# A fused attention and gated convolution kernel: the third weight unit loaded behind the first pair's queries and keys, with 30 GpSimd steps tied to VectorE

## The chip, the cores and the metric

The kernel runs on one core of a Trainium2 chip. The core has five engines with instruction queues of their own: TensorE (PE in the profile; PEld is its loading of weights), VectorE (DVE), ScalarE (ACT), GpSimd (POOL) and SyncE (SP), which here issues the transfers. The metric is the device time of one execution in microseconds. Of the kernel before, three runs are shown.

## What is computed

Attention inside chunks of 64 tokens, for 8 batches, 8 heads, 576 tokens and a head size of 64; its output, as rows of 512 numbers, goes through a causal convolution of five taps with a sigmoid (the gate), is multiplied by a weight matrix (the value), and the product of gate and value is multiplied by a second weight matrix:

```python
scores = scale * np.matmul(q_c, k_c.transpose(0, 1, 2, 4, 3))   # chunks of 64
scores = scores - np.max(scores, axis=-1, keepdims=True)
attn = np.exp(scores)
attn = attn / (np.sum(attn, axis=-1, keepdims=True) + 1e-09)
x = np.matmul(attn, v_c)                                        # then B x 576 x 512
for k in range(K):                                              # K = 5
    gate_pre += conv_w[k][None, None, :] * xp[:, k:k + S, :]
gate = 1.0 / (1.0 + np.exp(-gate_pre))
val = x @ w_val
return (gate * val @ w_out).astype(np.float32)
```

q, k and v are float32. The two weight matrices (512 x 512) and the taps are float64.

## The kernel before

**Tiling.** The 4608 tokens are cut into nine groups g of 512. In each group the eight heads make two pairs p of 128 partitions. Queries, keys and values of one (g, p) are 512 KB each, one tile of 128 x 1024 each; group 0's queries and keys of both pairs 0 1 and 0 0 come in halves b of 256 KB (S, mx and the like have a third number then). A weight matrix comes as four units of 128 rows, `v 0` to `v 3` of w_val and `o 0` to `o 3` of w_out, 512 KB each, since they are float64.

**What sets the order.** The program is one string, ORDER, of 1034 pieces. A loop takes them one by one and calls the function of each name; `run` (L138, L139, so every instruction of the kernel shows line L139) keeps this order on every engine. So each engine goes through its own instructions in the order of the string, waits where an input isn't ready, and what stands behind on that engine waits too. A table SLOTS says for every tile that a piece makes, one after the other, which buffer it takes: z for the 38 buffers of 128 x 1024 in SBUF, b for the four double banks of PSUM, e for two rows of exponentials. Buffers with a number from ALONE = 20 on lie in one tensor, `ys`; two neighbours there can be worked on by one instruction, where the code asks for a pair.

**The pieces.** `lq`, `lk`, `lv` load queries, keys and values of (g, p); `lw` loads a weight unit, `lc` the taps. All loads are issued by SP, in order. A weight unit's bits are turned on the chip into two float32 parts (`v_hi`, `v_lo`, `o_hi`, `o_lo`), in steps: w1, w3, w4, w7 on VectorE, w2, w5 and w6 on ScalarE, w8, wa and wb on GpSimd. Where `Q` is listed (`v 1`, `v 2`, `v 3`), the low part is summed on PE by three matmuls instead (wa and wb fall away) and copied by `wc` on ScalarE. A suffix D puts a step on VectorE, G on GpSimd.

For a pair: `S` makes scores on PE, `mx` their maxima (VectorE), `sb` subtracts (VectorE), `ex` is the exponential (ScalarE), `sm` sums and takes the reciprocal (VectorE), `nm` normalises (GpSimd), `T` transposes (PE), `ec` copies (ScalarE), `A` multiplies by the values (PE). There are two other ways to the exponentials. `ng` and `ea`: one exponential for each block of 64 on ScalarE, with the maximum as bias and the sum accumulated by it, 16 instructions for a pair and 8 for a half (`ra` and `rr`, or `rc`, then add a small number and invert). And `mh`, `M`, `exM`: the maxima in two parts (VectorE), subtracted on PE by matmuls into the scores, then one exponential out of PSUM.

`xr` and `xd` split the attention output into two parts (ScalarE, VectorE), `xc` copies it for the convolution, `k0`, `k`, `kk`, `kx` are taps, `sg` the sigmoid (ScalarE). `V g m c` is one contraction step of the value product, three matmuls of 512 columns (hi x hi, lo x hi, hi x lo); `vc` copies the value, `gs` multiplies it with the gate, `gr` and `gd` split that product, `P g m c` is a step of the out product, `oc` copies it and `st` stores. `W` are matmuls on zeros, `zr`, `zi`, `zw`, `zs` set constants up.

**Lines that matter here.** SLOTS and ALONE (L100), `run` (L138), `lw` (L183), `w1` (L203), `sc`, which is S (L261), `less`, which is M (L321), `exm` (L329) and the dispatch (L599 to L610).

## Time and profile before

| | |
|---|---|
| runs | 280.51, 281.16, 281.65 us (median 281.16) |
| span of the profiled execution | 279.6 us (of this execution the page gives the span alone) |
| PE busy | 268.9 us, 96% of the span, 3370 matmuls |
| PE loading weights | 216.6 us, 77% |
| VectorE busy | 239.5 us, 86%, 303 instructions |
| ScalarE busy | 198.7 us, 71%, 368 instructions |
| GpSimd busy | 59.4 us, 21%, 58 instructions |
| transfers | 42.46 MB, mean 152 GB/s |
| the chain that ended last | PE 89%, DMA 8% of the span |

The shares are means over the whole span. The page also has the span in 40 slices of 7 us; in it the second and third slice show PE at 5 and 9 tenths with transfers at 395 and 409 GB/s, and nearly every later slice shows PE at 9 tenths. So the table is read together with the chain of waits, which tells in which stage PE waits for transfers, and in which PE follows on itself.

### The profile page before, as it was taken

The numbers are of one execution on the slowest core, as the hardware profiler recorded it, in microseconds if no ns is written. First come the engines' busy times: TensorE is split into PE (matmuls) and PEld (weight loads), VectorE is DVE, ScalarE is ACT, GpSimd is POOL, SyncE is SP. The second block draws the span as 40 slices with busy tenths as digits, with TensorE's granted clock in tenths as the row PEclk, the third lists the DMA queues.
The fourth block names the chain that finished last, engine by engine and source line by source line (L and its number), as shares of the span: only waits on it lengthen the run. The fifth ranks groups of instructions, "written<-read, shape, count | busy, mean of one in ns | idle before, by whom it ended". The sixth has DMA issues, their size and how long they took to land.

```text
span 279.6 us, 7851 instructions
## 1 busy us (share of the span) xinstructions
PE 268.9 (96%) x3370; PEld 216.6 (77%) x3370; DVE 239.5 (86%) x303; ACT 198.7 (71%) x368; POOL 59.4 (21%) x58
## 2 busy tenths in 40 slices
PE   6598999999998999999999999999999999999995
PEld 3366778887886888888888888888888888888884
DVE  3979999999999988989898998999999998996020
ACT  5899999999997988895958588837644544614402
POOL 1056242049294003061335001100000000300000
PEclk9999999999999999999999999999999999999999
DMA  6999999763831649540082000000000000050656
GB/s 224 395 409 406 406 407 409 290 225 108 281 149 37 192 150 338 189 131 30 2 292 88 2 5 2 0 0 2 0 0 0 4 0 0 16 212 0 241 209 225
DMA packets 14754, 42.46 MB, mean 152 GB/s; under 512 B 1536, under 2 KB 1792, under 8 KB 14720
## 3 DMA queue, kind: packets, MB, share of 16 engines
q1 hardware_dynamic: 14720, 41.97, 40.7%
q8 instruction: 26, 0.43, 0.6%
q14 instruction: 8, 0.07, 0.1%
HBM read 32.53 MB, written 9.44 MB: 150 GB/s over the span
## 4 chain that ended last, share of the span: by engine, by line
PE 89%; DMA 8%; issue 1%; SPq 0%; ACT 0%
PE b L139 89%; DMA z<-in_v 4%; DMA z<-in_moe_w_val 2%; DMA z<-in_q 2%; SPq L139 0%; ACT z L139 0%
## 5 line engine op out<-in xcount | busy, mean ns | idle before, releaser
L139 PE MATMUL b<-z,v_hi 128*128 128x512 f32 x288 | 97.3, 403 | 1.3 <-issue 1.1
L139 PE MATMUL b<-o_hi,z 128*128 128x512 f32 (+1 forms) x296 | 94.5, 391 | 0.0
L139 DVE SCALAR_TENSOR_TENSOR ys<-ys,cw 128x511 f32<-128x511 f32 (+7 forms) x104 | 84.5, 863 | 0.1
L139 ACT COPY z<-b 128x1024 f32<-128x1024 f32 (+2 forms) x53 | 50.3, 970 | 38.3 <-PE b L139 35.5
L139 PEld LDWEIGHTS b<-z,v_hi 128*128 128x128 f32 x288 | 53.8, 188 | 14.5 <-issue 1.7
L139 PEld LDWEIGHTS b<-o_hi,z 128*128 128x128 f32 x296 | 55.1, 188 | 12.6
L139 PE MATMUL b<-o_lo,z 128*128 128x512 f32 (+1 forms) x148 | 57.4, 388 | 0.0
L139 PE MATMUL b<-z,v_lo 128*128 128x512 f32 x144 | 55.9, 394 | 0.0
L139 POOL TENSOR_TENSOR z<-e_row,rs 128x1024 f32<-128x1024 f32 (+1 forms) x15 | 27.0, 1804 | 47.2 <-DVE rs L139 17.0
L139 PEld LDWEIGHTS b<-o_lo,z 128*128 128x128 f32 x148 | 27.8, 188 | 5.9
L139 PEld LDWEIGHTS b<-z,v_lo 128*128 128x128 f32 x144 | 27.1, 188 | 5.4
L139 POOL TENSOR_TENSOR z<-ys,z 128x1024 fp32r<-128x1024 f32 x4 | 10.0, 2527 | 96.9 <-ACT z L139 96.9
L139 ACT ACTIVATE ys<-ys 128x1024 f32<-128x1024 f32 x16 | 16.8, 1059 | 11.0 <-DVE ys L139 10.8
L139 ACT ACTIVATE e_row<-b,mx 128x64 f32<-128x64 f32 x80 | 23.7, 345 | 0.4 <-DVE mx L139 0.4
L139 DVE TENSOR_TENSOR z<-b,z 128x1024 fp32r<-128x1024 f32 (+1 forms) x19 | 22.0, 1161 | 2.3 <-ACT z L139 1.3
L139 ACT CAST z<-ys 128x1024 fp32r<-128x1024 f32 x16 | 16.5, 1048 | 9.0 <-DVE ys L139 9.0
L139 DVE TENSOR_REDUCE mx<-b 128x16 f32<-128x1024 f32 (+1 forms) x19 | 21.6, 1144 | 1.3 <-PE b L139 1.1
L139 PEld LDWEIGHTS b<-z,z 64*64 64x64 f32 x960 | 15.7, 135 | 7.8 <-DMA z<-in_k 2.6
L139 PE MATMUL b<-z,z 64*64 64x64 f32 x960 | 17.6, 221 | 3.7 <-DMA z<-in_q 3.0
L139 ACT CAST z<-b 128x1024 fp32r<-128x1024 f32 (+1 forms) x19 | 18.7, 991 | 2.1 <-PE b L139 2.1
L139 ACT ACTIVATE ys<-ys,cw 128x512 f32<-128x512 f32 (+1 forms) x25 | 19.2, 811 | 0.0
L139 ACT ACTIVATION_READ_ACCUMULATOR e_row<-b,mx 128x1 f32 x80 | 19.0, 238 | 0.0
(74 smaller groups left out, 308.3 us busy)
## 6 DMA issues: line engine op xcount, KB each, us to landing
out<-z SPq DMA_DIRECT2D x16, 512.0 KB, 3.7
z<-in_q SPq DMA_DIRECT2D x10, 512.0 KB, 7.2
z<-in_v SPq DMA_DIRECT2D x9, 512.0 KB, 5.0
ys<-in_v SPq DMA_DIRECT2D x9, 512.0 KB, 10.1
ys<-in_k SPq DMA_DIRECT2D x9, 512.0 KB, 7.3
z<-in_k SPq DMA_DIRECT2D x7, 512.0 KB, 9.4
ys<-in_q SPq DMA_DIRECT2D x6, 512.0 KB, 10.2
z<-in_moe_w_val SPq DMA_DIRECT2D x4, 512.0 KB, 5.4
```

The lines of the kernel that those rows point to most:

```text
L139: return tc.keep_in_program_order(fn(*args, **kwargs))
```

## The change

The order string has 1033 pieces. The first 328 of them (up to about a third of the span) stand in another order than the first 329 of before; the last 705 are the same. What differs:

- `lw v 2`, the load of the third weight unit, stood third among the units; it now stands behind all queries and keys of the pairs 0 1 and 0 0. `lw v 0`, `lk 1 1` and `lq 1 1` stand later too, `lv 0 1` and `lv 0 0` earlier, and `lw o 0` is now among the first sixteen units.
- The two softmax halves 0 1 0 and 0 1 1 and the pair 2 1, which used `ea`, now use `mh`, `M`, `exM` (0 1 0) and `sb`, `ex` (0 1 1 and 2 1). The pair 1 0, which used `sb` and `ex`, uses `mh`, `M`, `exM`. A sum `sm` on VectorE replaces the accumulated one. This is 32 block exponentials fewer, and two `M`.
- Conversion steps change their engine: `w2 v 1` and `w2 v 3` from ScalarE to VectorE; `w6 v 0` and `w6 v 3` from VectorE to ScalarE; `w8 v 2` and `wa o 3` from VectorE to GpSimd; `w8 o 3` from GpSimd to VectorE; `w1` of `v 2`, `o 1` and `o 2` from VectorE to GpSimd; `w5` and `w8` of `v 0` become one VectorE step, `w58`; `xc 2 1` goes from VectorE to ScalarE.
- SLOTS gives other buffers to the tiles of the whole program; there are still 38 of z, and ALONE is 28 instead of 20, so `ys` holds 10 of them instead of 18. With this the last eight paired taps (`kk`, one instruction over two neighbours) become sixteen single ones.
- A table BEHIND lists 30 GpSimd pieces and a VectorE piece for each. The loop adds to the first instruction of the one a wait for the last instruction of the other. They are 12 `nm` (each behind the `sm` of its own pair), `nm 1 1` and `nm 3 1` behind taps, 4 `gd` and 12 conversion steps.
- Scores whose maximum is subtracted on PE start their accumulation only at the first of the blocks that share a bank (`start=` in `sc`).

```diff
-ORDER = """zw,lw v 1,zr 1,zr 0,lc,zi,zs 0,zs 1,lw v 3,lw v 2,w1 v 1,...
+ORDER = """lw v 1,w5 v 1,zr 1,zw,W 9 22,w3 v 1,w1 v 1,zr 0,lc,...
 ...
-ALONE = 20
+BEHIND = {
+    "w8 v 2": "w7 v 2", "nm 0 0": "sm 0 0", "wa v 0": "w58 v 0", "nm 1 0": "sm 1 0", "w1G o 2": "xd 0 0",
+    "nm 1 1": "k 0 3 3", "w8 o 0": "xd 1 0", "w8 o 2": "k 0 0 4", "nm 2 0": "sm 2 0", "w1G o 1": "mx 2 1",
+    "wa o 0": "k 0 1 3", "nm 2 1": "sm 2 1", "wa o 3": "gs 0 0", "nm 3 0": "sm 3 0", "wb o 3": "ng 3 1",
+    "nm 3 1": "k 1 1 2", "w8 o 1": "mx 4 1", "wa o 1": "xcD 3 0", "wb o 1": "sb 4 1", "nm 4 0": "sm 4 0",
+    "nm 4 1": "sm 4 1", "gd 1 1": "k 2 0 3", "gd 2 0": "nmD 5 1", "gd 2 1": "mx 6 0", "nm 6 1": "sm 6 1",
+    "nm 6 0": "sm 6 0", "nm 7 0": "sm 7 0", "nm 8 0": "sm 8 0", "nm 7 1": "sm 7 1", "gd 3 1": "k 8 2 2",
+}
+
+ALONE = 28
 ...
+    def w58(n, c, b=None):
+        run(V.scalar_tensor_tensor, out=rest(n, c, b)[1], in0=part(raw[n, c][0], b), scalar=2.0**-52,
+            in1=part(wt[n, c], b), op0=ALU.mult, op1=ALU.mult)
 ...
+        each, first = (g, p, b if own else None) not in LESS, own or (g, p) not in s_ps
 ...
-                            rhs=kk[r, b, c], start=True, stop=True, skip_group_check=True)
+                            rhs=kk[r, b, c], start=each or (first and u == a == 0), stop=True, skip_group_check=True)
 ...
+    on_gpsimd = dict(w1G=w1, w3G=w3)
 ...
+        begun = len(made)
 ...
+        ends[piece] = made[-1] if len(made) > begun else None
+
+        if piece in BEHIND:
+            sync = mybir.DependencyInfo(mybir.DependencyClass.Sync, mybir.DependencyReason.DATA)
+            tc.add_manual_dep(made[begun].ins, ends[BEHIND[piece]].ins.name, sync, reason="behind")
```

How the first loads stand on SP, before and then after; each list begins with v 3, the second weight unit. `in_moe_w_val 128x1024` is a weight unit of w_val, `in_k 128x512` and `in_q 128x512` are halves of keys and queries, 128x1024 whole ones.

```order
L139 DMA z1_90<-in_moe_w_val 128x1024
L139 DMA z2_92<-in_moe_w_val 128x1024
L139 DMA z6_152<-in_k 128x512
L139 DMA z7_154<-in_q 128x512
L139 DMA z9_181<-in_k 128x512
L139 DMA z6_152<-in_k 128x512
L139 DMA z7_154<-in_q 128x512
L139 DMA z10_185<-in_q 128x512
L139 DMA z9_181<-in_k 128x512
L139 DMA z10_185<-in_q 128x512
L139 DMA z11_268<-in_moe_w_val 128x1024
L139 DMA z12_270<-in_k 128x1024
```

```order
L147 DMA z3_126<-in_moe_w_val 128x1024
L147 DMA z4_129<-in_q 128x512
L147 DMA z5_139<-in_k 128x512 x2
L147 DMA z4_129<-in_q 128x512
L147 DMA z6_204<-in_k 128x512
L147 DMA z7_214<-in_q 128x512 x2
L147 DMA z6_204<-in_k 128x512
L147 DMA z8_266<-in_moe_w_val 128x1024
L147 DMA z2_281<-in_v 128x1024
L147 DMA z9_288<-in_q 128x1024
L147 DMA z10_290<-in_k 128x1024
L147 DMA z11_312<-in_moe_w_out 128x1024
```

The unit z2_92 of before, `v 2`, is z8_266 after: eight halves of queries and keys stand ahead of it, and values (z2_281) right behind it, which goes into the buffer of an earlier weight step.

On PE, around A 0 0 (writing b0_459 before and b2_437 after) and S 1 1 (b1_439 before, b0_477 after). Rows with `v_hi` and `v_lo` are parts of V pieces, the row with `ident` is T 0 0, `mr2_415` holds the maxima of the pair 1 0 for M 1 0.

```order
L139 MATMUL b0_419<-ident_62,z3_388 128x128 x8
L139 MATMUL b3_393<-z12_390,v_hi_67 128x512 x2
L139 MATMUL b3_393<-z12_390,v_lo_69 128x512
L139 MATMUL b1_439<-z13_373,z6_375 64x64 x16
L139 MATMUL b0_459<-z3_434,z7_377 64x64 x32
L139 MATMUL b1_439<-z13_373,z6_375 64x64 x16
```

```order
L147 MATMUL b2_405<-ident_62,z1_400 128x128 x8
L147 MATMUL b1_396<-z3_310,v_hi_67 128x512
L147 MATMUL b0_349<-mr2_415,signed_63 128x512 x4
L147 MATMUL b3_428<-z3_310,v_hi_67 128x512
L147 MATMUL b2_437<-z1_422,z13_430 64x64 x32
L147 MATMUL b3_428<-z2_344,v_hi_67 128x512
L147 MATMUL b1_396<-z3_310,v_lo_69 128x512
L147 MATMUL b1_396<-z3_310,v_hi_67 128x512
L147 MATMUL b1_396<-z3_310,v_lo_69 128x512
L147 MATMUL b0_477<-z14_435,z15_474 64x64 x32
```

S 1 1 stood half ahead of A 0 0 and half behind it; now both halves stand behind A 0 0, with V products between them and M 1 0 ahead.

On ScalarE, at the first softmaxes, before and after. `e_row0_65` holds the exponentials of the pair 0 1, `e_row1_66` those of 0 0; z1_303 is `w5` of the unit v 0, and z8_266 is the third weight unit, v 2.

```order
L139 ACTIVATE e_row0_65,rs1_197<-b1_164,mx1_191 128x64 x8
L139 ACTIVATE rs1_197<-rs1_197,e_row0_65 128x8
L139 ACTIVATE e_row0_65,rs2_278<-b0_211,mx2_246 128x64 x8
L139 ACTIVATE rs2_278<-rs2_278,e_row0_65 128x8
L139 ACTIVATE z1_303<-z11_268 128x512
L139 ACTIVATE e_row1_66<-e_row1_66 128x16x64
L139 CAST v_lo_69<-b1_289 128x2x256
L139 COPY z0_353<-b2_308 128x512
```

```order
L147 ACTIVATE e_row0_65<-b1_158 128x2x4x64
L147 ACTIVATE e_row0_65<-e_row0_65 128x2x4x64
L147 ACTIVATE z7_275<-z8_266 128x512
L147 COPY z4_277<-b2_270 128x512
L147 ACTIVATE z6_268<-z6_268 128x512
L147 ACTIVATE e_row1_66<-e_row1_66 128x16x64
L147 COPY z4_277<-b2_270 128x512
```

Sixteen block exponentials and two small additions became two exponentials over a half; w5 v 2 (into z7_275), the first copy of the transposed half and w2 v 2 (z6_268) now stand ahead of the exponential of the pair 0 0.

On GpSimd at the same place, before and after; the rows with `e_row` are `nm`.

```order
L139 TENSOR_TENSOR z0_106<-z0_106,z5_109 128x512
L139 TENSOR_TENSOR z9_296<-e_row0_65,rs1_197 128x2x256
L139 TENSOR_TENSOR z9_296<-e_row0_65,rs2_278 128x2x256
L139 TENSOR_TENSOR z3_388<-e_row1_66,rs3_333 128x1024
L139 TENSOR_TENSOR z1_303<-z1_303,z8_305 128x512
```

```order
L147 TENSOR_TENSOR z1_206<-z1_206,z0_153 128x512
L147 TENSOR_TENSOR z3_241<-e_row0_65,rs1_238 128x2x256
L147 TENSOR_TENSOR z3_241<-e_row0_65,rs2_244 128x2x256
L147 TENSOR_SCALAR z6_268<-z8_266 128x512
L147 TENSOR_TENSOR z7_275<-z7_275,z6_268 128x512
L147 TENSOR_TENSOR z1_400<-e_row1_66,rs3_322 128x1024
```

Between the `nm` of the second half and that of the pair 0 0 there are now two steps of the third weight unit, w1G v 2 (the TENSOR_SCALAR) and w8 v 2.

## Rows read from the trace of the kernel before

**Rows 1.** The chain of waits in order of time: start us, us, what.

```profile
2.10 6.26 DMA z<-in_moe_w_val
...
8.38 5.37 DMA z<-in_q
...
13.77 11.88 DMA z<-in_v
...
25.78 5.95 PE b L139 x118
...
84.78 0.90 issue
...
276.70 0.37 ACT z L139
```

**Rows 2.** Windows: stretch, us, each engine's busy us (instructions), PEclk, DMA share, GB/s.

```profile
7.00:28.00 21.00, 16.46 (x422) 11.59 (x422) 18.26 (x37) 19.04 (x58) 7.97 (x7) 1.00 1.03 403
27.49:68.75 41.26, 41.09 (x723) 33.38 (x724) 39.56 (x60) 40.33 (x102) 16.04 (x11) 1.00 0.81 313
```

**Rows 3.** Timeline of PE: start us, us, what, [idle before, releaser].

```profile
8.04 0.40 PE L139 MATMUL b<-z,signed 128*128 128x512 f32 x1
...
24.66 0.69 PE L139 MATMUL b<-z,z 64*64 64x64 f32 x32
...
25.78 1.63 PE L139 MATMUL b<-z,z 64*64 64x64 f32 x96 [0.43 <-DMA z<-in_v]
...
32.69 0.86 PE L139 MATMUL b<-z,v_hi 128*128 128x512 f32 x3
33.39 0.39 PE L139 MATMUL b<-z,v_lo 128*128 128x512 f32 x1
...
35.56 1.16 PE L139 MATMUL b<-z,z 64*64 64x64 f32 x64
36.65 0.97 PE L139 MATMUL b<-z,v_hi 128*128 128x512 f32 x3
```

**Rows 4.** Timeline of SP's issues near 15 us.

```profile
15.10 0.33 SPq L139 DMA_DIRECT2D z<-in_v  x1
```

**Rows 5.** Transfers, four stretches: KB and us to landing; packets, MB, share of queues.

```profile
z<-in_v SPq DMA_DIRECT2D x1, 512.0 KB, 11.8
...
q8 instruction: 1, 0.02, 1.7%
...
q8 instruction: 1, 0.02, 1.9%
...
q8 instruction: 1, 0.02, 5.5%
```

**Rows 6.** Timeline of GpSimd.

```profile
1.10 0.29 POOL masks.py:199 TENSOR_SCALAR_AFFINE_SELECT ident<-ident 128x128 f32<-128x128 f32 x1
...
14.17 1.27 POOL L139 TENSOR_TENSOR z<-z,z 128x512 fp32r<-128x512 f32 x1 [12.78 <-ACT e_row L139]
15.39 1.04 POOL L139 TENSOR_TENSOR z<-e_row,rs 128x512 f32<-128x512 f32 x1
...
20.58 1.90 POOL L139 TENSOR_TENSOR z<-e_row,rs 128x1024 f32<-128x1024 f32 x1 [1.55 <-PE b L139]
...
242.40 2.91 POOL L139 TENSOR_TENSOR z<-ys,z 128x1024 fp32r<-128x1024 f32 x1 [66.32 <-ACT z L139]
```

**Rows 7.** Timeline of ScalarE.

```profile
17.68 1.04 ACT L139 ACTIVATE e_row<-e_row 128x1024 f32<-128x1024 f32 x1
...
19.09 0.59 ACT L139 COPY z<-b 128x512 f32<-128x512 f32 x1
```

**Rows 8.** Timeline of VectorE.

```profile
18.82 1.24 DVE L139 TENSOR_REDUCE rs<-e_row 128x16 f32<-128x1040 f32 x1 [0.92 <-ACT e_row L139]
...
242.29 4.90 DVE L139 SCALAR_TENSOR_TENSOR z<-tails,cw,z 128x512 f32<-128x512 f32 x4
...
248.25 2.85 DVE L139 SCALAR_TENSOR_TENSOR z<-tails,cw,z 128x512 f32<-128x512 f32 x4
```

## The prediction

> **What bounds the kernel now.** I read the chain of waits first, in order of time [rows 1]. It has two parts. Up to 25.8 us it runs through transfers: the third weight unit until 2.10 + 6.26 = 8.36 us, then queries until 13.75, then the values that A 0 0 needs, which land at 13.77 + 11.88 = 25.65. From 25.78 the chain is TensorE (PE) alone to 276.70, but for 0.90 us at 84.78, in which PE waited for nothing that the profile shows. The windows say the same [rows 2]: from 7 to 28 us PE is busy 16.46 of 21 us, 4.5 us idle, with the transfer engines full at 403 GB/s; from 27.5 to 68.75 it is busy 41.09 of 41.26. Behind the start PE is never idle for lack of work, so a later stage is worth nothing as long as its results come before PE wants them. So the question is one number: **how much useful PE work is done when PE stops waiting for loads.** The granted clock is 1.00 in both windows.

> **The break-even.** The last load that PE waits for is different in the two kernels. Before, the first half of S 1 1 starts at 24.66, then PE idles 0.43 us, and A 0 0 starts at 25.78 [rows 3]. In the new order A 0 0 stands ahead of S 1 1, and S 1 1 is the last piece whose load can be late. What stands ahead of S 1 1 there and not here: A 0 0, which takes 36.65 - 35.56 = 1.09 us in a dense stretch, and three more V products (eight against five) at (33.39 - 32.69) / 3 = 0.233, together 0.70 [rows 3]. So a start of S 1 1 at 24.66 + 0.43 + 1.09 + 0.70 = **26.88 us** gives the old time, and each microsecond earlier or later is one of the total, if nothing waits behind it.

> **When S 1 1 can start: the loads.** The queue is in order, and landings follow the bytes ahead. In units of 512 KB the old order has 15 units up to the values of A 0 0 and 16 up to the next values; the new one has 14 up to the values of A 0 0 and 16 up to the queries of S 1 1. The sixteenth unit of before was issued at 15.10 and took 11.8 [rows 4, 5]: it landed at 26.9. The seventh landed at 8.38 + 5.37 = 13.75 [rows 1], so nine units took 13.15 us. At 403 GB/s [rows 2] a unit takes 1.30 us and nine take 11.7, so some 1.5 us were lost to transfer engines that ran behind the others; in the same stretch instruction packets went through the same engines [rows 5]. Landing of the sixteenth unit in the new kernel: 25.4 with none of this loss, 26.9 with all of it. The new order doesn't starve the queue: the values that go into a buffer of the first weight unit's steps wait for products that end near 8.4 us (8.04 + 0.40 [rows 3]), and some four units are then still queued ahead.

> **When S 1 1 can start: the computed chain.** Here the new order gains early and gives it back. (1) The first unit's sum ends as before, at 8.4. The two halves for S 0 1 0 are now the third unit, whose landing was 8.36 [rows 1], so S 0 1 0 starts at 8.45; S 0 1 1, one unit later, about 9.75. (2) The two softmax halves: maxima, the four new M products (256 columns, 0.5 us), exponentials, sums on VectorE; then two GpSimd multiplies of 1.04 us each [rows 6]. The first ends near 14.0, the second near 15.05, so T 0 1 1 is done at 15.7. (3) Now ScalarE's queue: behind the copy for T 0 1 0 stands w2 v 2, which waits for w1G v 2, a GpSimd tensor-scalar that the old trace doesn't hold. **Its price** lies between 0.29 us (GpSimd's select on 128x128) and 1.90 (its 1024-wide multiply); I take 1.28, that of its 512-wide multiplies, since the size is the same [rows 6]. It ends at 15.05 + 1.28 = 16.35. Queued behind it on ScalarE are w2 v 2 (taken as 0.65), ex 0 0 (1.04) and the copy for A 0 1 1 (0.59) [rows 7], with overlaps done at 18.5. (4) A 0 1 1 ends at 19.2, S 1 0 at 20.3. (5) The third unit: sum of ex 0 0 on VectorE (1.24 [rows 8]) and its reciprocal to 19.6, nm 0 0 on GpSimd 1.90 [rows 6] to 21.55; w6 v 2 on ScalarE to 20.5, so Q v 2 runs 20.55 to 22.0. (6) T 0 0, three V products and M 1 0 (0.93) follow to 24.65; the copy of T 0 0 is ready at 24.35. A 0 0: 24.65 to 25.7. Four V products: **26.6 us**. At the other price ends of w1G this is 25.6 and 27.2.

> S 1 1 starts at the later of the two, 26.6 to 26.95. I take 26.75, between the full loss and none of the loss on the loads, with the chain as it is: a gain of 0.13 us. All the PE work that the change adds (two M pieces, 1.4 us) lies ahead of S 1 1 and is in this sum.

> **The rest, part by part.** It costs nothing on PE as far as I can see. ScalarE loses 32 of its 80 exponentials with accumulation and gets one-piece exponentials and a few copies: less work. VectorE: in the stretch from mx 1 1 to mx 4 0 (27.49 to 68.75) it is busy 39.56 of 41.26 us [rows 2], so it is nearly a second bound. There the new order takes nine steps out (xd 0 0, xcD 2 1, waD o 3, four w1 and w3, rc and ng: 4.8 us start to start) and puts three in (sb 2 1, sm 2 1, w8D o 3: 3.2 us), but starts 0.8 us later, since S 1 1 ends later. It comes out about 0.8 us ahead. The new buffers turn the last eight paired taps into sixteen single ones near 180 us: between nothing (the same columns) and 8 x 0.71 = 5.7 us (a tap of [rows 8]) more on VectorE; I take 1 us, nearer to nothing since the columns are the same, and count on the results lying ahead of their readers. **The ties:** 14 of 30 name a step that GpSimd needs or must await anyway (twelve nm behind sm, w8 v 2, wa v 0) and add nothing. The other 16 hold a GpSimd step until a named VectorE step ends; queued behind each are only GpSimd's own later steps, and PE waits for them last in nm 1 1, about 1 us ahead of T 1 1. What such a tie can be worth shows late in the trace: four taps took 4.90 us while GpSimd's 2.91 us subtraction ran, and 2.85 us alone [rows 6, 8].

> [...]

> **The rivals.**
> (a) *Faster by more than 0.5%.* The loads lose nothing (25.4) and w1G is cheap (chain 25.6 to 25.9): S 1 1 at 25.9 gives 1.0 us; and the 0.90 us stall at 84.78, ahead of which an instruction packet was carried [rows 5], falls elsewhere because 8 more products stand ahead of it. Both: 281.16 - 1.9 = 279.3. For it: the loss is not regular. Against it: both have to come together.
> (b) *Slower: VectorE comes late.* Between 28 and 69 us VectorE has under 1 us to spare for PE: by my sum xd 1 1 ends some 0.4 us before V 1 3 2 wants it, and nm 1 1 can't start until k 0 3 3 ends. A GpSimd step that runs beside taps costs VectorE 2.05 us [rows 8]. It decides once VectorE loses over 0.5 us there; one such loss gives 281.16 + 1.55 = 282.7, and it isn't won back, since PE has no idle time to give. For it: the sum is tight; against: the ties avoid just these meetings.
> (c) *The clock falls.* The three filler products (W 3) move ahead of the first sum, and PE is as thinly used from 8.5 to 15 us as it was. [...] Against it: it stayed 1.00 with 4.5 us of 21 idle [rows 2]. [...]
> (d) *The change doesn't do what it says*: the moved unit's lead is eaten by the next loads, as the queue is full either way. That is most of my forecast.

> **How the numbers follow.** Forecast: 281.16 - 0.13, **281.0 us**. The span is 279.6 against a median of 281.16, so 1.6 us lie around it, and I leave them as they are; the runs shown spread 280.51 to 281.65. The forecast's own range, from chain and load ends (S 1 1 at 25.9 to 27.2, a gain of 1.0 or a loss of 0.3) with 0.9 us for the stall either way: 279.9 to 282.1. Chances: forecast 0.57, (a) 0.23, (b) 0.15, (c) 0.05. About 0.5% (1.4 us) is what a measurement of this kernel can tell from no change: faster 0.23, same 0.57, slower 0.20. The range reaches into (a) and (b): 279.3 to 282.8.

> **What would show it.** Right: S 0 1 0 near 8.45, w1G v 2 near 1.3 us, S 1 1 behind a wait of 0 to 0.4 us at 26.6 to 27.0, PE without gaps after it. Wrong: S 1 1 before 25.9 or after 27.5; any PE wait on VectorE between 28 and 70 us; a granted clock under 1.00 after 5 us; V products of group 1 waiting for xd 1 1.

## The result: slower by half a per cent, and the profile after

| | before | changed |
|---|---|---|
| median of 20 runs | 281.25 us (280.07 to 281.96) | 282.55 us (281.39 to 284.26) |
| ratio | | 1.0052, 95% interval 1.0035 to 1.0068 |
| span of the profiled execution | 279.6 us | 280.9 us (its time: 282.70 us) |
| mean granted clock of the profiled execution | 1.000 | 0.994 |

I had forecast 281.0 us, a gain of 0.13. The measured time lies inside my range of 279.3 to 282.8, but the kernel became slower, not faster, and the whole interval of the ratio lies above 1. Ratios leave out executions more than 1.5% above the fastest of their kernel: below, one of e3's six, three of e5's nine and three of e11's six, and the profiled executions of e5 and e11 are among these.

The mean clock of the 20 executions of the changed kernel is 1.000 in 6 (median 281.78 us) and between 0.980 and 0.994 in 14 (median 282.93). So part of the loss goes with the clock, and part is there without it. The lower clock isn't new in kind: of 74 executions of the kernel before that ran beside the experiments, 32 lay below 0.998, at a median of 281.2 us against 280.8 for the others.

The page of the changed kernel has, at its head:

```profile
PE 272.3 (97%) x3378; PEld 219.5 (78%) x3378; DVE 241.4 (86%) x312; ACT 191.9 (68%) x306; POOL 59.9 (21%) x61
...
PEclk9979999999999999999999999999999999999999
```

PE has 3.4 us more busy time than before, and the third slice of 7 us, from 14 to 21 us, shows a clock of 7 tenths. The timeline of PE there (start us, us, what, idle time before and its releaser):

```profile
12.23 1.42 PE L147 MATMUL b<-z,z 64*64 64x64 f32 x64 [0.65 <-ACT e_row L147]
14.48 0.66 PE L147 MATMUL b<-ident,z 128*128 128x128 f32 x4 [0.83 <-POOL z L147]
15.90 0.67 PE L147 MATMUL b<-ident,z 128*128 128x128 f32 x4 [0.77 <-ACT z L147]
...
17.57 2.07 PE L147 MATMUL b<-z,ident 128*128 128x512 f32 x2
18.65 1.34 PE L147 MATMUL b<-v_hi,signed 128*128 128x512 f32 x1
19.83 0.39 PE L147 MATMUL b<-z,signed 128*128 128x512 f32 x1
...
28.10 1.16 PE L147 MATMUL b<-z,z 64*64 64x64 f32 x64
...
31.76 0.77 PE L147 MATMUL b<-ident,z 128*128 128x128 f32 x5 [0.34 <-issue]
32.28 0.94 PE L147 MATMUL b<-z,v_hi 128*128 128x512 f32 x3
```

The sum of v 3 (17.57 to 20.22) takes 2.65 us; I had counted 1.45 for such a sum. A 0 0 starts at 25.88, S 1 1 at 28.10 instead of 26.75, and no load is waited for there any more. The windows of that stretch (stretch, us, each engine's busy us, PEclk, DMA share, GB/s) give the cause:

```profile
14.00:16.50 2.50, 1.25 (x8) 0.84 (x8) 2.46 (x4) 1.69 (x3) 2.04 (x3) 0.97 1.03 406
16.50:17.57 1.07, 1.07 (x34) 0.95 (x33) 0.93 (x3) 1.07 (x3) 0.00 (x0) 0.50 1.01 394
17.57:20.30 2.73, 2.73 (x16) 1.32 (x16) 1.82 (x3) 1.08 (x4) 1.27 (x1) 0.60 1.03 414
```

From 16.5 us the granted clock is 0.50. Ahead of it PE is busy for half of 2.5 us, in two short pieces.

Then there is the end of that timeline: at 31.76, in the middle of T 1 0, PE has been idle for 0.34 us for "issue", that is for nothing the profile shows. The kernel before has the same at 31.90, with 0.17 us, besides the 0.90 us at 84.78 that I had read [rows 1]. These small rows turned out to be half of the story.

### The profile page after: what moved, and what is told of

Same layout as the page of the kernel before. It is cut to its first block, busy times and chain, and to the rows that moved or that the text cites. A ratio compares the mean times of both kernels' runs of the same rounds, so it can differ in the third digit from the quotient of the medians.

```text
span 280.9 us, 7812 instructions
## 1 busy us (share of the span) xinstructions
PE 272.3 (97%) x3378; PEld 219.5 (78%) x3378; DVE 241.4 (86%) x312; ACT 191.9 (68%) x306; POOL 59.9 (21%) x61
## 4 chain that ended last, share of the span: by engine, by line
PE 71%; issue 0%; ACT 0%
PE b L147 71%; ACT z L147 0%
## 5 line engine op out<-in xcount | busy, mean ns | idle before, releaser
L147 ACT COPY z<-b 128x1024 f32<-128x1024 f32 (+2 forms) x64 | 60.5, 963 | 36.1 <-PE b L147 35.4
L147 PEld LDWEIGHTS b<-o_hi,z 128*128 128x128 f32 x296 | 55.1, 188 | 12.6
L147 DVE SCALAR_TENSOR_TENSOR z<-z,cw,z 128x511 f32<-128x511 f32 (+3 forms) x80 | 55.8, 738 | 0.0
L147 POOL TENSOR_TENSOR z<-z,z 128x1024 fp32r<-128x1024 f32 (+2 forms) x9 | 16.3, 1813 | 113.5 <-PE b L147 67.9
L147 ACT ACTIVATE z<-z 128x1024 f32<-128x1024 f32 (+3 forms) x25 | 21.2, 859 | 19.5 <-DVE z L147 16.0
L147 DVE SCALAR_TENSOR_TENSOR ys<-ys,cw 128x1022 f32<-128x1022 f32 (+7 forms) x32 | 31.0, 1003 | 0.0
L147 DVE TENSOR_TENSOR z<-z,z 128x1024 f32<-128x1024 f32 (+3 forms) x22 | 25.2, 1169 | 1.9 <-PE b L147 1.3
L147 PEld LDWEIGHTS b<-z,z 64*64 64x64 f32 x1216 | 20.0, 137 | 6.0 <-issue 3.7
L147 PE MATMUL b<-z,z 64*64 64x64 f32 x1216 | 22.4, 223 | 1.4 <-DMA z<-in_q 0.7
L147 PE MATMUL b<-ident,z 128*128 128x128 f32 x144 | 19.2, 275 | 1.9 <-POOL z L147 0.8
L147 PEld LDWEIGHTS b<-ident,z 128*128 128x128 f32 x144 | 16.4, 140 | 4.5 <-POOL z L147 1.9
## 6 DMA issues: line engine op xcount, KB each, us to landing
z<-in_q SPq DMA_DIRECT2D x9, 512.0 KB, 10.5
```

Of the source, the lines that this page charges most:

```text
L147: made.append(tc.keep_in_program_order(fn(*args, **kwargs)))
```

## Experiments

All ratios are against the kernel before, run on the same chip beside the experiment; "changed" is the changed kernel.

### e1: fillers in PE's gaps

```diff
-S 0 0 1,sm 0 1 0,
+W 2,S 0 0 1,sm 0 1 0,
-w1G v 2,T 0 1 0,
+w1G v 2,W 3,T 0 1 0,
-ex 0 0,T 0 1 1,
+ex 0 0,W 3,T 0 1 1,
```

> The changed kernel with eight matmuls on zeros added in three idle gaps of PE: two ahead of S 0 0 1 (11.6 us), three ahead of T 0 1 0 (13.7) and three ahead of T 0 1 1 (15.1). Nothing else differs. Clock theory: the loss comes from the granted clock, which in the changed kernel stood at 0.50 from 16.5 us, behind a stretch in which PE worked only in short pieces with 0.65 to 0.83 us of idleness between them; A 0 1 0, the sum of v 3 and with them all that follows ended 1.2 us later than they would at 1.00. With the gaps filled the mean clock is 1.000 in all executions (0.980 to 0.994 in 14 of 20 executions of the changed kernel), the sum of v 3 takes about 1.5 us instead of 2.65, and the time falls by some 0.8 us, to a ratio of 1.001 to 1.003 against the kernel before. Rival, the chain: the softmax chain alone makes S 1 1 late, and the clock's dip lies in its shadow; then the clock rises to 1.000 and the ratio stays at 1.005 or goes up by up to 0.003, since the fillers can only add work.

Measured: 282.57 us, ratio 1.0060 (1.0034 to 1.0086). The mean clock was 0.999 or 1.000 in 5 of 7 executions (all were expected), and the time stayed. In the timeline of PE the first half of the theory holds (S 1 1 is the row at 26.43), and then the gain is lost in one gap:

```profile
26.43 1.16 PE L139 MATMUL b<-z,z 64*64 64x64 f32 x64
27.52 0.96 PE L139 MATMUL b<-z,v_lo 128*128 128x512 f32 x3
30.34 1.09 PE L139 MATMUL b<-z,v_hi 128*128 128x512 f32 x4 [1.86 <-issue]
```

S 1 1 came 1.67 us earlier than in the changed kernel, and 1.86 us of "issue" follow. The windows show that in this gap every other engine went on:

```profile
28.50:30.30 1.80, 0.00 (x0) 0.00 (x0) 1.80 (x4) 1.78 (x4) 0.99 (x2) 1.00 1.01 401
```

So the clock theory is right about S 1 1 and wrong about the end. The rival named the right ratio, but for a reason that the rows don't show: nothing of the softmax chain is late.

**A new theory: blocks of PE instructions.** The windows from the start to the end of this gap count the instructions that PE had by then (matmuls, then weight loads): before to 31.90, changed to 31.76, e1 to 30.34.

```profile
0.00:31.90 31.90, 25.04 (x474) 16.69 (x474) 24.47 (x50) 26.81 (x71) 10.46 (x15) 1.00 0.95 364
...
0.00:31.76 31.76, 27.09 (x473) 18.10 (x473) 24.93 (x52) 21.40 (x36) 11.69 (x17) 0.95 0.94 360
...
0.00:30.34 30.34, 25.41 (x471) 16.23 (x474) 25.09 (x53) 21.57 (x36) 11.70 (x17) 1.00 0.95 360
```

It is the same number in three kernels whose pieces differ (the trace of e1 lacks two matmul records): with the few semaphore instructions, PE instruction 960 to 963. And in each, PE goes on 2.4 to 2.5 us after the start of a 16 KB packet on queue q8, which the transfers view calls "instruction":

| kernel | packet starts | PE goes on | later by | idle before | in which piece |
|---|---|---|---|---|---|
| before | 29.39 | 31.90 | 2.51 | 0.17 | V 0 0 0 2 |
| changed | 29.32 | 31.76 | 2.44 | 0.34 | T 1 0 |
| e1 | 27.92 | 30.34 | 2.42 | 1.86 | V 0 3 2 2 |

So the theory is that PE gets its instructions in blocks, each with one such packet, and waits at the end of a block until the next is there. No view shows what a packet holds; below, "block" and "boundary" stand for this reading of the counts.

### e2: no ties

```diff
-BEHIND = { ... }
+BEHIND = {}
```

> The changed kernel without its 30 waits of GpSimd on VectorE; order, buffers and loads are the same. Theory of the clock: the ties have no part in the loss; the mean clock still falls to about 0.994 in most executions, ratio 1.003 to 1.007. Rival, the ties: a GpSimd step that is held back makes PE late; without them the ratio falls to 1.000 or below. Other rival, the ties protect VectorE: without them GpSimd runs beside VectorE's steps in the dense stretch from 28 to 70 us, VectorE falls behind, PE waits for xd or a copy, and the ratio rises above 1.008.

Measured: 283.22 us, ratio 1.0067 (1.0044 to 1.0090), clock 0.994 in 6 of 8 executions, as the theory of the clock expected. The ties do not make the loss. Whether they help can't be told from this ratio; the intervals of e2 and of the changed kernel overlap. See e9.

### e3: the moved load put back

```diff
-lw v 3,w3 c 0,
+lw v 3,lw v 2,w3 c 0,
 ...
-mx 0 0,lw v 2,w1G v 2,
+mx 0 0,w1G v 2,
```

> The changed kernel with only the load of v 2 put back, directly behind that of v 3, so that all halves of queries and keys land 1.28 us later; the steps on all engines stand as in the changed kernel. This prices the moved load by itself. If the head start is worth what I counted, S 0 1 0 starts near 10.1 instead of 8.88 and the softmax chain ends 1.2 us later, and PE is idle 1.2 us more ahead of it: the ratio rises to 1.009 to 1.011, and the clock falls as often or oftener than in the changed kernel. Rival: the chain is set behind the halves by something else (the load of the queries and keys of the pairs 1 0 and 1 1, or the sum of v 2), and the ratio stays within 0.002 of 1.005.

Measured: 286.53 us, ratio 1.0166 (1.0121 to 1.0211), above the expected 1.009 to 1.011. In the profiled execution the clock was 0.998 and the time 282.94 us; in the other five it was 0.974 to 0.976 and the time 286.45 to 287.31. So the load order matters, and the largest losses go with the clock; of those five executions there is no trace. The trace there is shows what the load costs while the clock stays up (1.00 to 35 us, without fillers):

```profile
28.42 1.16 PE L138 MATMUL b<-z,z 64*64 64x64 f32 x64
...
14.00:16.50 2.50, 1.50 (x65) 1.32 (x66) 2.43 (x6) 1.37 (x3) 1.64 (x3) 1.00 1.00 406
16.50:17.57 1.07, 0.51 (x4) 0.27 (x3) 1.04 (x2) 0.53 (x1) 1.07 (x2) 1.00 1.03 417
```

S 0 1 0 started at 10.76 there, behind 1.53 us of waiting for its keys, and S 1 1 is the row at 28.42. The other two rows will matter at the end: PE is thinly used here, and the clock did not fall.

### e4: the sum of v 3 ahead of T 0 1 0

```diff
-w1G v 2,T 0 1 0,
+w1G v 2,Q v 3,T 0 1 0,
 ...
-w7 v 2,Q v 3,wc v 3,
+w7 v 2,wc v 3,
```

> The changed kernel with one piece moved on PE: the sum of v 3 (Q v 3, 1.45 us at full clock) stands ahead of T 0 1 0 instead of behind A 0 1 0; its inputs are there at 12.6 us. PE has 0.83 and 0.77 us of idleness at that place. Clock theory: real work fills the gaps, the mean clock is 1.000, and in place of the 2.65 us of the slowed sum only what does not fit into the gaps is paid: S 1 1 starts near 26.2 instead of 28.1, ratio 0.995 to 0.999. Rival, the chain: T 0 1 0 starts 0.6 us later, and since the copies and A 0 1 0 follow from it, all of it is passed on; the clock may rise, but the ratio stays above 1.002.

Measured: 281.92 us, ratio 1.0019 (1.0000 to 1.0038), clock 0.998 to 1.000 in 10 of 12 executions. Real work kept the clock up here, as the fillers did in e1 (0.999 or 1.000 in 5 of 7). S 1 1 started at 27.34, not 26.2, and 0.70 us of "issue" stood ahead of 31.35, 2.49 us after a packet at 28.86. The expected 0.995 to 0.999 was missed, by the block and by a slower start (S 0 1 0 at 9.53, behind 0.59 us of waiting for its keys).

### e5 to e8: fewer and more PE instructions

The row of fillers at PE's very start is changed, `W 9 22` being 9 matmuls of 512 columns and 22 of 64:

```diff
-W 9 22
+W 12          (e5, in the changed kernel; e6, in e1; e7, in the kernel before)
+W 6 44        (e8, in the changed kernel)
```

> The changed kernel with a shorter row of filler matmuls at its very start: 12 of 512 columns in place of 9 of 512 and 22 of 64, about as long in time, but 19 matmuls (38 PE instructions) fewer. Theory of the program's blocks: PE's instructions come from memory in blocks, and near PE instruction 961 of every kernel so far PE stood idle, waiting for nothing else, until 2.4 to 2.6 us after the start of a 16 KB instruction packet (before 31.90 us, changed 31.76, the filled one 30.34). With 38 instructions fewer ahead, 19 more matmuls of the same work lie ahead of that boundary: the idle time of 0.34 us at 31.4 goes, and in executions in which the granted clock stays up more of it; ratio 1.001 to 1.004 (1.005 for the changed kernel). Rival: the idle time belongs to the piece (T 1 0) or to the transfers at that time; then it stays at that piece and the ratio stays near 1.005.

> The kernel with the filled gaps (eight fillers in the idle gaps of PE between 11 and 15 us) and with the shorter row at the start (19 matmuls fewer). The filled kernel alone had the clock at 1.000 and S 1 1 at 26.43 instead of 28.10, and then stood idle for 1.86 us at 28.5. Theory of the program's blocks: the boundary now lies 11 matmuls further on than in the changed kernel and 19 further than in the filled one; PE gets there after 31 us, when the block is there; the idle 1.86 us go, and the span falls from 280.8 to about 279.0, ratio 0.997 to 1.000. Rival, the idle 1.86 us are a wait for data or a cost of the fillers: they stay, ratio 1.005 to 1.007.

> The kernel before with the same shorter row at the start (12 wide fillers, 19 matmuls fewer). Theory of the program's blocks: it waits only 0.17 us at this boundary, since its other waits (loads until 25.8) let the block arrive in time; it gains 0.2 us at most there, and the 0.90 us at 84.8, which lie at PE instruction 3010, move to another piece and may shrink; ratio 0.996 to 1.000. Rival: the row itself is worth something (clock or start), then this kernel gains as much as the two others.

> The changed kernel with a row of the same length in time but more instructions at its start: 6 fillers of 512 columns and 44 of 64 in place of 9 and 22, 19 matmuls (38 PE instructions) more. Nothing else differs. Theory of the program's blocks: the boundary falls into S 1 1, which PE reaches near 28.5; the block is there at 30.3 at the earliest (as in the filled kernel) and at 31.8 if the packet comes when it does in the changed kernel; so PE stands idle for 1.4 to 2.8 us there, and the ratio rises to 1.009 to 1.014. Rival: idle time belongs to the piece or the transfers; ratio stays near 1.005.

| | time | ratio, interval | mean clock |
|---|---|---|---|
| e5, changed, 38 PE instructions fewer | 283.74 us (all nine) | 1.0061 (1.0028 to 1.0094) | below 0.998 in 8 of 9 |
| e6, filled, 38 fewer | 280.16 us | 0.9977 (0.9966 to 0.9989) | 0.999 or 1.000 in 11 of 11 |
| e7, before, 38 fewer | 280.62 us | 0.9989 (0.9975 to 1.0002) | below 0.998 in 7 of 12 |
| e8, changed, 38 more | 285.26 us | 1.0165 (1.0140 to 1.0191) | below 0.998 in 4 of 5 |

e8 is the clearest: the boundary at instruction 962 fell into S 1 1, as expected, after 55 of its 64 matmuls, at the same count (473 matmuls by 31.87 us) and 2.43 us after a packet at 29.44.

```profile
18.27 0.39 PE L139 MATMUL b<-z,z 64*64 64x64 f32 x10 [1.07 <-issue]
...
29.63 1.04 PE L139 MATMUL b<-z,z 64*64 64x64 f32 x55
31.87 0.35 PE L139 MATMUL b<-z,z 64*64 64x64 f32 x9 [1.20 <-issue]
...
0.00:31.87 31.87, 24.65 (x473) 16.74 (x473) 23.66 (x50) 19.52 (x32) 10.84 (x16) 0.95 0.94 362
```

Its time is above the expected 1.009 to 1.014. The first row shows what the expectation had left out: PE also stood for 1.07 us at instruction 450, until 2.38 us after a packet at 15.89.

e6 is the counterpart: the clock is steady, PE passes the boundary without idle time, and nothing of the gain is lost. Its S 1 1 and what follows:

```profile
26.60 1.16 PE L139 MATMUL b<-z,z 64*64 64x64 f32 x64
...
29.42 1.04 PE L139 MATMUL b<-ident,z 128*128 128x128 f32 x8
```

S 1 1 at 26.60 is the value of my chain. e6 is faster than both kernels; no "issue" of 0.1 us or more is left in its trace, not even at 84.78, where the kernel before has its 0.90 us. e7 gains 0.1% from the shorter row (its interval goes from 0.25% to nothing). Run side by side, e6 is 0.46 us faster than e7 by the medians. That is what the new order gave once its two obstacles were gone, but not its worth alone: e7's profiled execution has an obstacle of its own, 0.78 us at instruction 1474.

e5 missed its expectation of 1.001 to 1.004. In its profiled execution the idle time at instruction 962 is gone, but later boundaries are hit instead: 0.49 us at instruction 1218, and the worst at instruction 1474, 2.36 us after a packet at 45.81:

```profile
48.17 1.14 PE L139 MATMUL b<-z,z 64*64 64x64 f32 x33 [3.10 <-issue]
```

The clock fell there behind the 3.10 us, not ahead of it: it was 1.00 from 14 to 48 us and 0.57 from 48 to 52. That execution took 285.92 us, against 281.47 of the fastest, so it doesn't show what the others lost. Moving the boundaries was no cure by itself: e5 is not faster than the changed kernel.

### e9 to e11: the parts of the change with the clock held

e9 is e6 without the ties, e10 is e6 with the load of v 2 put back as in e3. e11 is the changed kernel with `W 12`, the sum of v 3 early as in e4, `W 2` ahead of S 0 0 1 and of T 0 1 1.

> The filled and shortened kernel (ratio 0.9977 with the clock at 0.999 or above in all executions) without the 30 waits of GpSimd on VectorE. With the clock steady this shows the ties alone. My prediction: they are worth nothing to the sum, since PE waits for neither side; ratio 0.997 to 0.999. Rival, the ties protect VectorE from GpSimd's steps in SBUF: without them VectorE falls behind between 28 and 77 us and PE waits; ratio 0.999 to 1.003. Other rival, they hold GpSimd back and cost: ratio below 0.9965.

Measured: 280.65 us, ratio 0.9991 (0.9968 to 1.0013); e6 had 0.9977 (0.9966 to 0.9989) on another occasion. As times these are not told apart, and the interval holds both my 0.997 to 0.999 and the 0.999 to 1.003 of the rival that the ties protect VectorE. The traces show one thing, twice: S 4 1 0, near 76 us, waits 1.10 us for exponentials in e9 (1.09 in e2) and 0.50 in e6 (0.50 in the changed kernel). The rows point to `ng 3 1` on VectorE, a step on 128x16, which the tie `wb o 3` behind `ng 3 1` lets go first. First VectorE and GpSimd in e9, then the same two steps in e6:

```profile
69.36 0.75 DVE L132 TENSOR_SCALAR mx<-mx 128x16 f32<-128x16 f32 x1
...
68.79 1.29 POOL L132 TENSOR_TENSOR o_lo<-z,z 128x512 fp32r<-128x512 f32 x1
```

```profile
68.60 0.17 DVE L139 TENSOR_SCALAR mx<-mx 128x16 f32<-128x16 f32 x1
...
68.84 1.29 POOL L139 TENSOR_TENSOR o_lo<-z,z 128x512 fp32r<-128x512 f32 x1 [0.77 <-DVE mx L139]
```

Without the tie the VectorE step started second, at 69.36 against 68.79, and ended only when GpSimd's did, at 70.11 against 70.08; it took 0.58 us longer than alone in e6, and PE waited for its result.

> The filled and shortened kernel with only the load of v 2 put back, directly behind that of v 3. With the clock steady this prices the moved load by itself. If the head start of 1.28 us reaches the dense stretch, S 1 1 starts 1.0 to 1.3 us later than 26.60 and the ratio rises to 1.001 to 1.003. Rival: as in my prediction's case (d), the lead is eaten by the next loads and by the block of PE instructions, which comes when it comes; then the ratio stays below 1.000. If the longer idleness ahead of S 0 1 0 brings the clock down in spite of the fillers, mean clocks of 0.975 as in the unfilled kernel with this load order show it, and the ratio is above 1.005.

Measured: 282.06 us, ratio 1.0045 (1.0020 to 1.0069), clock 0.987 to 0.994 in all 6. The fillers did not hold the clock here: S 0 1 0 waits 1.69 us for its keys, and the windows show the clock down behind it (0.53 from 14 to 16 us):

```profile
14.00:16.00 2.00, 2.00 (x65) 1.74 (x64) 1.66 (x4) 0.60 (x2) 0.75 (x1) 0.53 1.03 414
```

S 0 1 0 starts 1.41 us later than in e6 (10.34 against 8.93) and S 1 1 2.15 us later (28.75). The lead and the clock can't be parted by this run, but e3's trace parts them: with the clock at 1.00 S 0 1 0 started there at 10.76 and S 1 1 at 28.42, 1.8 to 2.0 us behind the 26.43 to 26.60 of the three kernels with fillers and the moved load. So, in that one execution, the lead of the moved load reached S 1 1; it was not eaten by the next loads.

> The changed kernel with the shorter row at the start, and with real work in place of most fillers: the sum of v 3 stands ahead of T 0 1 0 (1.45 us of work in a gap that held 0.8 us of fillers), two fillers stand ahead of S 0 0 1 and two ahead of T 0 1 1. A 0 1 1 then starts about 0.9 us earlier; the sum of v 2 follows its own inputs (19.2 us and the copy w6), so 0.3 to 0.9 us of it stay. Expected: S 1 1 at 25.9 to 26.4 (its queries land near 25.9), ratio 0.995 to 0.9975. Rival, the blocks of PE instructions: PE then gets earlier to the boundaries near instructions 450, 706 and 962, waits there until 2.4 us after the packets of about 16, 22 and 28 us, and the ratio stays at 0.9975 to 0.999 with idle time at these places.

Measured: 282.46 us (all six, from 279.67 to 287.87), ratio 0.9971 (0.9938 to 1.0004) from three of them. Its best executions (279.67 and 280.06 us) are as good as e6's; in the profiled one PE waited 3.08 us at instruction 1474, as in e5. So it stays inconclusive.

### e12: the clock held, the blocks where they were

```diff
-W 9 22
+W 9 14        (with the eight fillers of e1: as many PE instructions as the changed kernel)
```

> The changed kernel with the eight fillers in PE's gaps, and eight of the 22 narrow fillers of the first row taken out, so that PE has as many instructions as in the changed kernel and its blocks end at the same pieces. This takes the clock's dip away and leaves the blocks where they are. If both the clock and the blocks make the loss, S 1 1 starts near 26.5, PE reaches T 1 0 near 30 us and waits there for the block near instruction 962, until 2.4 us after a packet of 27.9 to 28.5, that is 30.3 to 30.9; the ratio is 0.9985 to 1.001, between the changed kernel (1.005) and the filled and shortened one (0.998). Rival, the clock alone is the cause and the filled kernel's loss was the fillers' own: then the ratio is 0.998 or below. Rival, the blocks alone: then it stays at 1.004 or above, with 1 us or more of idle time at the boundary.

Measured: 281.59 us, ratio 1.0023 (1.0003 to 1.0044), clock 1.000 in 11 of 12. S 1 1 at 26.52; PE reaches T 1 0 and waits in its middle, where the changed kernel does, now 2.54 us after a packet at 27.95:

```profile
26.52 1.16 PE L139 MATMUL b<-z,z 64*64 64x64 f32 x64
...
30.49 0.66 PE L139 MATMUL b<-ident,z 128*128 128x128 f32 x4 [0.55 <-issue]
...
84.38 0.94 issue
```

The median lies a little above the forecast band, and the interval reaches into it. The first rival (0.998 or below) is outside the interval; the second (1.004 or above) touches its upper end, but its 1 us or more at that boundary isn't there. The steps are then 1.0052 (changed), 1.0023 (clock held) and 0.9977 (clock held and blocks in time). The last step holds two boundaries: the last row, from the chain, is a wait of 0.94 us at instruction 3010, where the changed kernel has 0.45 and e6 none.

## Why the prediction was wrong

**The loads: right.** The sixteenth unit was issued at 15.40 and landed 10.5 us later, near 25.9 (25.4 to 26.9 forecast), and S 1 1 did not wait for it. What the 1.5 us between those bounds were lost to before, no row shows.

**The chain: right at full clock, in part by luck.** S 0 1 0 started at 8.88 (8.45 forecast; the sum of v 1 and the keys were both later). The multiplies ended 0.4 us later than forecast, and w1G v 2 took 0.65 us, the lower part of my bounds of 0.29 to 1.90, where I had taken 1.28; the two cancel.

```profile
13.38 2.04 POOL L147 TENSOR_TENSOR z<-e_row,rs 128x512 f32<-128x512 f32 x2 [0.79 <-ACT e_row L147]
15.39 0.65 POOL L147 TENSOR_SCALAR z<-z 128x512 f32<-128x512 f32 x1
```

With the clock held, S 1 1 came at 26.43, 26.60 and 26.52 (e1, e6, e12): the forecast was 26.6. Two of its own signs of being wrong came in the changed kernel: S 1 1 after 27.5, and a clock under 1.00.

**The clock: the first step that failed.** The sum had it at nothing, and the rival (c) had a chance of 0.05; by the mean clock it came true in 14 of 20 executions, of which one has a trace. I had argued that the clock had stayed at 1.00 with 4.5 us of 21 idle [rows 2]. That was the wrong row to argue from. Over 7 to 14 us the changed kernel's PE is even busier than before (5.16 us against 4.09); what differs is the next stretch. Before, the sums of v 2 and v 3 stand there, and the windows of that kernel show PE busy without a gap:

```profile
14.00:17.00 3.00, 3.00 (x39) 1.87 (x39) 2.47 (x4) 2.94 (x20) 2.27 (x2) 1.00 1.03 410
```

The change moves both sums behind 17.5 us and leaves 1.25 us of work in 2.50. The new order thus took away the work that had filled this place: the sum of v 2 with its load, and the sum of v 3 by its place in the string, for e4 could put it back. S 1 1 came 1.5 us later for it (28.10 against 26.60). No row of the kernel before could price it, since its clock was 1.00 in all windows there; in the changed kernel's trace it was 0.50 from 16.4 to 19.7 us. By my own break-even this alone turns the gain of 0.13 us into a loss of 28.10 - 26.88 = 1.22 us, near the 1.30 us between the medians.

**The break-even: the second step that failed.** "A start of S 1 1 at 26.88 us gives the old time, and each microsecond earlier or later is one of the total, if nothing waits behind it." Something waits behind it: PE stood idle for "issue" there, 1.86 us in e1 and 0.55 us in e12. e1 has S 1 1 0.45 us ahead of that point and e12 0.36 us, and both were slower than the kernel before (1.0060 and 1.0023). The right place to compare the two orders is PE instruction 962, where both kernels stand idle for "issue", before until 31.90 (0.17 us), changed until 31.76 (0.34 us). In front of it the old order has done 19 V products and all of T 1 0; the new one 15 V products and three of the eight transposes, since the eight matmuls of M 0 1 0 and M 1 0 have taken their places in the count. Still to do are then 4 x 0.233 = 0.93 us [rows 3] and, from the rows at 31.76 and 32.28 above, 0.52 us of transposes. 0.93 + 0.52 - 0.14 = **1.31 us**; the spans differ by 280.9 - 279.6 = 1.3.

The clock and the blocks are not two terms to be added: in the changed kernel PE is slow to the boundary (clock) and waits only 0.34 us there; with the clock held it gets there earlier and waits 0.55 (e12) or, with more instructions ahead, 1.86 us (e1). So the 1.22 us and the 1.31 us are the same loss, counted at S 1 1 and at the boundary.

**The stall at 84.78: half seen.** I had named an instruction packet beside it [rows 5] and left its 0.90 us to chance. It lies at PE instruction 3010 = 962 + 8 x 256, where PE goes on 2.45 us after a packet at 83.23. In the changed kernel it is 0.45 us (85.72 in the chain), and a wait of 0.50 us for exponentials at 77.11 makes up for it.

```profile
85.68 191.00 PE b L139 x1883
...
85.72 0.45 issue
86.17 191.79 PE b L147 x1892
```

The first row is the kernel before, the others are the changed one. From that instruction on PE follows on itself in both, and the 0.79 us more are the nine matmuls that the new order has still to do. So the new buffers and the sixteen single taps cost PE nothing there; no run tested them by themselves.

**The ties and VectorE: nearly right.** In the changed kernel's trace the only wait of PE between 28 and 70 us is the 0.34 us for "issue", none for VectorE, so rival (b) did not come. That the ties are worth "nothing to the sum", as e9 expected, was wrong for one tie out of 30, which by the traces saves PE 0.6 us at 76 us; the times don't tell it apart.

**The range.** Its terms, added up plainly, give 281.16 - 1.0 - 0.9 = 279.3 to 281.16 + 0.3 + 0.9 = 282.4; the narrower 279.9 to 282.1 is not that sum, and how it was formed isn't said.

**What stays open:** what starts an instruction packet, and so why it comes at 27.9 in e1 and e12 and at 29.3 in the changed kernel; why PE stood for 3.10 and 3.08 us at instruction 1474 in the profiled executions of e5 and e11; and why the kernel before loses so little at a mean clock of 0.994 (in e7's trace the clock was down from 11.0 to 14.5 us, and PE still waited for others behind it, busy for 8.08 of the next 9.20 us). Open, too, is why the clock falls in some executions of a kernel and not in others.

## What to carry to other kernels

Idle time "for issue" on the engine that bounds a kernel is worth a look even at 0.2 us: count the instructions ahead of it in two versions. Here the count was the same, 960 to 963, in three kernels whose pieces differed, and e1, whose S 1 1 ahead of it came 1.67 us earlier than that of the changed kernel, took the same time (282.57 against 282.55 us); so compare two orders at such a count, not at a piece. And before work is moved out of a thin stretch of TensorE, ask what keeps the engine busy there afterwards: here the clock was then a term of the sum, about 1.2 us, not a rival with a small chance.

## What the runs showed of the hardware

**The granted clock fell to 0.50 behind gaps of at most 0.83 us** in the changed kernel, where PE had been busy for 1.25 of 2.50 us; with fillers in the same gaps (2.18 of 2.50 in e1) it stayed at 1.00. Such gaps did not bring it down every time: it stayed at 1.00 in e3's trace, with 1.50 of 2.50 and 0.51 of the next 1.07 us busy, behind a wait of 1.53 us, and the changed kernel itself had 1.000 in 6 of 20 executions.

**A tiny VectorE step took 0.75 us beside a GpSimd step, and 0.17 us alone:** the one on 128x16, which started 0.57 us behind a GpSimd step of 1.29 us in e9 and ended with it, and in e6 ended before that step started (68.77 against 68.84).
